# Moving the loads of a fused attention and MLP kernel to ScalarE's queue, the tail's exponentials to SBUF, and respacing the row-sum inverses

## The chip, the cores and the metric

The kernel runs on one NeuronCore of a Trainium2 chip. The core has five instruction streams that run side by side and meet at semaphores: TensorE (PE: matmuls, and PEld for its weight loads), VectorE (DVE), ScalarE (ACT), GpSimd (POOL) and SyncE (SP), which here only issues DMAs. Sixteen DMA engines move the data. The metric is the device time of one execution in microseconds (us); lower is better.

## The reference, cut to what matters

Attention over 4 batches, 8 heads, 576 positions and head size 64 with rotary positions, then a gated MLP with a mixing matrix over the positions, then a low-rank mixer and a wide MLP. The change lies in the attention.

```python
def _attn_ref(q, k, v):
    B, H, S, D = q.shape              # 4, 8, 576, 64
    ...
    q_rot, k_rot = (rotate(q), rotate(k))
    scores = (1.0 / np.sqrt(D)) * np.matmul(q_rot, k_rot.transpose(0, 1, 3, 2))
    scores = scores - np.max(scores, axis=-1, keepdims=True)
    attn = np.exp(scores)
    attn = attn / (np.sum(attn, axis=-1, keepdims=True) + 1e-09)
    return np.matmul(attn, v)

def _moe_ref(x, w_in, g_ln, w_sg, b_sg, w_out):
    h = gelu(x @ w_in); u, v = split(h)
    v_s = w_sg @ layernorm(v) * g_ln + b_sg
    return x + (u * v_s) @ w_out

def _moe2_ref(x, U, V, w_ch1, w_ch2):
    u = x + ((x.T @ U) @ V).T
    return u + np.maximum(u @ w_ch1, 0.0) @ w_ch2
```

The weights of the MLPs come as float64 and are turned to float32 on the chip.

## The kernel before

The attention runs head by head, 32 heads, in an order that is written by hand for all five engines. Time is counted in **ticks**: in each tick TensorE does one chunk `c` of 128 keys of one head `h` (five chunks a head, the fifth, the **tail**, has 64 keys), so head `h` has the ticks 5h to 5h + 4. In a tick `t` stand, in this order: the scores of chunk `t` (`scores`, four matmuls into a PSUM tile `st`), work left over for VectorE from the tick before (`lows`), one chunk of the row maxima of a head some ten ticks ahead (`row_max`, two matmuls into a PSUM tile `sm`, and VectorE's maximum over it into `MX`, L222), the product of the exponentials with the values of three ticks ago (`values`, L281), and then all that `later(t, ...)` has put down for this tick. Each engine works off its own list strictly in that order. `st` and `sm` share three PSUM buffers, so TensorE can write a new one only when ScalarE has taken the exponentials of an `st`, or VectorE the maximum of an `sm`, two or three tiles back.

What the change touches:

- **Loads.** `load(h)` (L138) brings the raw keys and queries of a head, 576 KB, at tick 5h - 30 into one of four buffers; `load_v(i)` (L143) brings the values of a pair of heads, in two transfers, at tick 10i - 16; `converted` (L348) brings a chunk of float64 weights (512 KB for most), one each 13 ticks, which ScalarE and VectorE convert from five ticks later on, one operation a tick (L71 to L75). All are issued by SP.
- **SP's other work** in the attention: copies that stack the rotated keys and queries on both halves of the partitions (`Q<-K`, `K<-K`, L164 to L170), a constant row (L174), the row of maxima that `scores` needs in its second two matmuls (`Q<-mt`, L226, issued when a head's maxima are all there, some four ticks ahead of its scores), and the inverses' four steps below. SP takes them in their order too: one that waits holds up all behind it.
- **Rotation.** GpSimd turns the raw keys and queries (`rope`, L149 to L151) from tick 5h - 23 on and makes the low part of the split keys (L168).
- **The tail's exponentials** (`scores`, L251 to L260). Four chunks of five go from PSUM through ScalarE's exponential to SBUF. The tail's are kept more precisely, as a rounded part and a rest: ScalarE takes the exponential in place in PSUM (L252), copies it rounded to SBUF (L254), and VectorE subtracts the two (L260) at the start of the next tick.
- **The inverses of the row sums** (`finish`). When the odd head of a pair is done, at tick t0 (10i + 12 for pair i), ScalarE has both heads' results in SBUF (`stage`, five buffers, L297). SP gathers their sums into a 128-partition tile (`collect`, rc, L312, at t0); `INVERSE = 4, 6, 9, 14` sets the ticks after t0 of the rest: GpSimd adds 1e-9 (L315), VectorE inverts (L318) and SP writes the result to DRAM (rr, L319), SP reads it back to 64 partitions (rb, L324), VectorE multiplies both heads by it (`apply`, L331, in two ticks).

After the attention come the MLP stages, in which Tile's scheduler orders all engines but TensorE.

Of the kernel before, what the change touches and what calls it, by code (L numbers as in the profile page):

```python
# [40 lines left out]

AHEAD, RAMP_FROM, RAMP, MAX_1, ROW, ROW_0, ROW_1 = 10, -1, 25, -1, 2, -8, -9

INVERSE = 4, 6, 9, 14

MATRIX, APART, CONVERT, ROWS = 12, 13, 5, (151, 159)

# [5 lines left out]
def tile_kernel(ctx: ExitStack, tc: tile.TileContext, qk, vv, tabs, w_in, g_ln, wsgT, b_sg, w_out, u_r, v_r, w1, w2, out):  # L53
# [32 lines left out]
    D = 64  # L86
# [48 lines left out]
    VSs = [p1.tile([P, 2, len(SPLITS), D + 1], F32R, name=f"VS_{i}") for i in range(4)]  # L135

    def load(h):
        nc.sync.dma_start(RAW[h % NR], qk[h // NHEAD, h % NHEAD].rearrange("c p s -> p c s"))  # L138

    def load_v(i):  # L140
        b, pr = divmod(i, NPAIR)
        for a in range(2):
            nc.sync.dma_start(VVs[i % 3][:, :, a, :D], vv[b, pr, :, :, a, :])  # L143

    def rope(e, h):

# [91 lines left out]
    def scores(h, c):  # L238
        kk = TS[c]
        K1, Q1, K2, Q2 = (t[h % NS] for t in (K1s, Q1s, K2s, Q2s))  # L240
        ps = psp.tile([P, 2, 512], F32, tag="ss", name=f"st{h}_{c}", bufs=3)
        for l, r, st in ((K1, Q1, True), (K2[0:D + 1], Q2, False)):
            for n in range(2):
                ns = slice(n * HALF, (n + 1) * HALF)
                nc.tensor.matmul(ps[:kk, n, :HALF], l[:, c * P:c * P + kk], r[:, ns], start=st, stop=not st)  # L245
        if c not in SPLITS:
            pc = p1.tile([P, S], F32, tag="pc", name=f"pc{h}_{c}", bufs=4)
            nc.scalar.activation(h2(pc[:kk]), ps[:kk, :, :HALF], AF.Exp, scale=0.125)  # L248
            PCS[h, c] = pc
            return  # L250
        pc = ps[:kk, :, :HALF]  # L251
        nc.scalar.activation(pc, pc, AF.Exp, scale=0.125)  # L252
        ph = p1.tile([P, S], F32R, tag="ph", name=f"ph{h}_{c}", bufs=3)
        nc.scalar.activation(h2(ph[:kk]), pc, AF.Copy)  # L254
        if kk == P:
            pl = p1.tile([P, S], F32R, tag="pl", name=f"pl{h}_{c}", bufs=2)
        else:
            pl = ph[D:P]
        PCS[h, c] = ph, pl
        lows.append(lambda: nc.vector.tensor_tensor(h2(pl), pc, h2(f(ph[:kk])), ALU.subtract))  # L260

    def values(h, c, t0):
        if c == 0:
# [3 lines left out]
        for n in range(2):  # L267
            ns = slice(n * HALF, (n + 1) * HALF)
            o = PVS[h][:D + 1, n, :HALF]
            if c in SPLITS:  # L270
                VS = VSs[h % 4]
                j = SPLITS.index(c)
                ph, pl = pc
                if kk == P:
                    pr = [(VS[:, 0, j], ph[:, ns]), (VS[:, 1, j], ph[:, ns]), (VS[:, 0, j], pl[:, ns])]
                else:
                    pr = [(VS[:, 0, j], ph[:, ns]), (VS[:, 1, j], ph[:, ns])]
            else:
                pr = [(VVs[(h // 2) % 3][:kk, c, h % 2], pc[:kk, ns])]
            for j, (l, r) in enumerate(pr):  # L280
                nc.tensor.matmul(o, l, r, start=(c == 0 and j == 0), stop=(c == NC - 1 and j == len(pr) - 1))  # L281
# [6 lines left out]
    def finish(h, t0):  # L288
# [27 lines left out]

        def invert():
            nc.vector.reciprocal(rc, rc)  # L318
            nc.sync.dma_start(rr, rc)  # L319

        def spread():
# [11 lines left out]
        def apply_last():  # L333
            nc.vector.tensor_tensor(X[b][:, pr], X[b][:, pr], RB[i], ALU.mult)
        later(t0, collect)
        for tick, fn in zip(INVERSE, (guard, invert, spread)):
            later(t0 + tick, fn)
        if i < NP - 1:
            for a in range(2):
                later(t0 + INVERSE[3] + a, lambda a=a: apply(a))  # L340
        else:
            later(t0 + INVERSE[3], apply_last)

    def converted(t0, src, n, use):

        raw = p1.tile([P, 512, 2], U32, tag="raw64", name="raw64", bufs=1)[:, :n]
        t = p1.tile([P, 512], F32, tag="t64", name="t64", bufs=1)[:, :n]
        later(t0, lambda: nc.sync.dma_start(raw.rearrange("p n w -> p (n w)"), src))  # L348
        for j, fn in enumerate(from_f64(t, raw) + use(t)):
            later(t0 + CONVERT + j, fn)  # L350

# [572 lines left out]
```

## Time and profile before

| | |
|---|---|
| median of 3 runs | 973.37 us (969.28 to 974.08) |
| the profiled execution | 976.05 us, span 974.0 us |
| busy share of the span | PE 96%, PEld 84%, DVE 53%, POOL 39%, ACT 35% |
| attention | some 12 to 325 us of the span |
| DMA engines, mean busy share | 0.54 to 0.75 in each 40 us up to 280 us |
| granted TensorE clock | 0.989 in the mean |

A row of the timeline is: start in us from the span's start, duration in us, engine, line, operation, out<-in, and in brackets the idle time before it with what ended it. SPq, ACTq and the like are an engine's sequencer: there the duration of a DMA row is the time that issuing took, not the transfer. The durations of single matmuls overlap, so that TensorE's pace is read from the distance between equal instructions of two heads and not from their sum.

### The profile page before, as it was taken

What the parts mean: (1) busy time and instruction counts of PE and PEld (TensorE: products, weight loads), DVE (VectorE), ACT (ScalarE), POOL (GpSimd) and SP (SyncE); (2) the same over time, 40 slices, a digit from 0 to 9 for tenths busy, and PEclk for the clock granted to TensorE, in tenths of its full rate; (3) what the DMA queues carried; (4) which work ended last, traced back from release to release, by engine and by line L of the source; (5) the groups of instructions that cost most, each with busy time, mean ns of one, the idle gap of its engine ahead of it and who ended that gap; (6) DMA issues with size and microseconds to landing.
All of it is one profiled execution on the core that took longest, in us unless ns stands there. A gap on an engine that the chain in (4) does not pass through costs nothing.

```text
span 974.0 us, 13234 instructions
## 1 busy us (share of the span) xinstructions
PE 938.5 (96%) x5211; PEld 817.4 (84%) x5212; DVE 515.3 (53%) x721; ACT 343.6 (35%) x549; POOL 377.1 (39%) x325
## 2 busy tenths in 40 slices
PE   6899988989999999999999899999999999999998
PEld 2687766767787898999999798899889988998897
DVE  7667776777775377344327946642552542212222
ACT  4466654655666463323215423221321221010010
POOL 7767866777761586231427533210210120000000
PEclk8999999999999999999999999999999999999999
DMA  5568676767751500000003001220220110000112
GB/s 177 143 181 199 174 178 160 206 158 172 190 128 49 159 28 1 1 1 1 23 22 109 23 23 60 91 66 1 87 87 1 65 44 1 1 1 21 60 40 75
DMA packets 58948, 78.00 MB, mean 80 GB/s; under 512 B 31403, under 2 KB 35270, under 8 KB 58886
## 3 DMA queue, kind: packets, MB, share of 16 engines
q1 hardware_dynamic: 58886, 77.16, 28.9%
q8 instruction: 41, 0.67, 0.3%
q14 instruction: 21, 0.17, 0.1%
HBM read 55.02 MB, written 4.79 MB: 61 GB/s over the span
## 4 chain that ended last, share of the span: by engine, by line
PE 76%; DVE 11%; DMA 5%; issue 3%; POOL 1%; SPq 1%; ACT 1%; DVEq 0%; ACTq 0%; POOLq 0%
PE a L551 21%; PE r L551 20%; PE pv L281 11%; PE st L245 6%; PE w L551 5%; PE sm L217 3%; PE m L551 3%; PE u L551 3%; PE v L551 3%; DVE MX L222 2%; DVE t L75 1%; DVE t L74 1%; DMA raw<-in_qk 1%; DMA g<-in_wsgT 1%; DVE t L72 1%
## 5 line engine op out<-in xcount | busy, mean ns | idle before, releaser
L222 DVE TENSOR_REDUCE MX<-sm 128x1 f32<-128x576 f32 (+1 forms) x160 | 119.3, 749 | 68.2 <-PE sm L217 42.1
L281 PE MATMUL pv<-pc,VV 128*65 128x288 f32 x512 | 146.7, 410 | 0.9 <-ACT stage L297 0.5
L245 PE MATMUL st<-Q,K 65*128 65x288 f32 (+3 forms) x640 | 126.7, 320 | 10.0 <-DVE MX L222 4.2
L245 PEld LDWEIGHTS st<-Q,K 65*128 65x128 f32 (+3 forms) x640 | 96.3, 180 | 24.4 <-DVE MX L222 7.3
L743 ACT ACTIVATE RH<-r 128x944 fp32r<-128x944 f32 (+1 forms) x38 | 35.7, 939 | 211.4 <-PE r L551 211.4
L744 DVE SCALAR_TENSOR_TENSOR RL<-r,RH 128x944 fp32r<-128x944 f32 (+1 forms) x38 | 42.4, 1117 | 126.3 <-ACT RH L743 126.2
L248 ACT ACTIVATE pc<-st 128x576 f32<-128x576 f32 x128 | 82.7, 647 | 66.8 <-PE st L245 63.6
L551 PE MATMUL a<-RH,setB 128*128 128x472 f32 (+1 forms) x320 | 95.6, 371 | 0.0
L281 PEld LDWEIGHTS pv<-pc,VV 128*65 128x65 f32 x512 | 69.1, 138 | 30.9 <-issue 1.0
L759 DVE TENSOR_TENSOR X<-a,X 128x416 f32<-128x416 f32 (+4 forms) x65 | 46.4, 745 | 91.0 <-PE a L551 91.0
L217 PE MATMUL sm<-K,Q 128*128 128x288 f32 (+1 forms) x320 | 78.3, 329 | 13.7 <-DVE MX L222 5.9
L551 PE MATMUL a<-RH,setA 128*128 128x472 f32 (+1 forms) x288 | 86.1, 370 | 0.0
L551 PE MATMUL r<-UH,setB 128*128 128x472 f32 (+1 forms) x256 | 76.4, 369 | 0.0
L551 PE MATMUL r<-UH,setA 128*128 128x472 f32 (+1 forms) x256 | 76.2, 370 | 0.0
L217 PEld LDWEIGHTS sm<-K,Q 128*128 128x128 f32 (+1 forms) x320 | 52.4, 184 | 22.9 <-DVE MX L222 8.1
L551 PEld LDWEIGHTS a<-RH,setB 128*128 128x128 f32 x320 | 60.2, 188 | 6.9
L515 POOL TENSOR_TENSOR setB<-t,setB 128x512 fp32r<-128x512 f32 x16 | 20.7, 1292 | 103.0 <-ACT setB L704 60.4
L551 PE MATMUL a<-RL,setB 128*128 128x472 f32 (+1 forms) x160 | 59.6, 372 | 0.0
L551 PEld LDWEIGHTS a<-RH,setA 128*128 128x128 f32 x288 | 54.1, 188 | 6.1
L551 PE MATMUL a<-RL,setA 128*128 128x472 f32 (+1 forms) x144 | 53.4, 371 | 0.0
L551 PEld LDWEIGHTS r<-UH,setA 128*128 128x128 f32 x256 | 48.1, 188 | 5.2
L551 PEld LDWEIGHTS r<-UH,setB 128*128 128x128 f32 x256 | 48.0, 188 | 5.2
(172 smaller groups left out, 1957.6 us busy)
## 6 DMA issues: line engine op xcount, KB each, us to landing
raw<-in_qk SPq DMA_DIRECT2D x31, 576.0 KB
Q<-K SPq DMA_DIRECT2D x87, 144.0 KB
raw<-in_w SPq DMA_DIRECT2D x24, 512.0 KB
VV<-in_vv SPq DMA_DIRECT2D x32, 160.0 KB
rb<-rr SPq DMA_DIRECT2D x15, 288.0 KB
K<-K SPq DMA_DIRECT2D x29, 144.0 KB
raw<-in_w_in SPq DMA_DIRECT2D x8, 512.0 KB
gt<-in_w SPq DMA_DIRECT2D x8, 512.0 KB
```

Of the source, the lines that this page charges most:

```text
L72: lambda: nc.vector.tensor_scalar(t, t, F64_LEAST, F64_MOST, ALU.max, ALU.min),
L74: lambda: nc.vector.scalar_tensor_tensor(tu, hi, 0xC0000000, tu, ALU.bitwise_and, ALU.bitwise_or),
L217: nc.tensor.matmul(ps[:TS[t], n, :HALF], Q1[:, t * P:t * P + TS[t]], K1[:, n * HALF:(n + 1) * HALF], start=True, stop=True)
L222: nc.vector.tensor_reduce(MXs[h % 2][:TS[t], t:t + 1], ps[:TS[t], :, :HALF], AX.XY, ALU.max)
L245: nc.tensor.matmul(ps[:kk, n, :HALF], l[:, c * P:c * P + kk], r[:, ns], start=st, stop=not st)
L248: nc.scalar.activation(h2(pc[:kk]), ps[:kk, :, :HALF], AF.Exp, scale=0.125)
L281: nc.tensor.matmul(o, l, r, start=(c == 0 and j == 0), stop=(c == NC - 1 and j == len(pr) - 1))
L515: return nc.gpsimd.tensor_tensor(out, a, b, ALU.subtract)
L551: nc.tensor.matmul(o, l, rr, start=(j == 0), stop=(j == n - 1))
L743: nc.scalar.activation(RH[:, s], ps[:, :, :WIDE[blk]], AF.Relu)
L744: nc.vector.scalar_tensor_tensor(RL[:, s], ps[:, :, :WIDE[blk]], 0.0, f(RH[:, s]), ALU.max, ALU.subtract)
L759: nc.vector.tensor_tensor(X[b][:, e2, xs], ps[:, :n, us], X[b][:, e2, xs], ALU.add)
```

## The change

Three things change. `load` from head 4 on, `load_v` from pair 2 on, and the loads of `converted` are issued by ScalarE in place of SP; they stand in ScalarE's list where they stood in SP's, at the end of their tick. The tail's exponential goes to a new SBUF tile `pt` (one buffer) instead of back to PSUM; the rounded copy and the subtraction then read `pt`, and `ph` has two buffers in place of three. The inverses' steps after `collect` come 6, 8, 9, 12 and 17 ticks after t0: the write to DRAM (`gather`) is a step of its own, one tick behind the inversion.

```diff
--- before.py
+++ after.py
@@ -41,7 +41,7 @@
 
 AHEAD, RAMP_FROM, RAMP, MAX_1, ROW, ROW_0, ROW_1 = 10, -1, 25, -1, 2, -8, -9
 
-INVERSE = 4, 6, 9, 14
+INVERSE = 6, 8, 9, 12, 17
 
 MATRIX, APART, CONVERT, ROWS = 12, 13, 5, (151, 159)
 
@@ -135,12 +135,12 @@
     VSs = [p1.tile([P, 2, len(SPLITS), D + 1], F32R, name=f"VS_{i}") for i in range(4)]
 
     def load(h):
-        nc.sync.dma_start(RAW[h % NR], qk[h // NHEAD, h % NHEAD].rearrange("c p s -> p c s"))
+        (nc.scalar if h >= NR else nc.sync).dma_start(RAW[h % NR], qk[h // NHEAD, h % NHEAD].rearrange("c p s -> p c s"))
 
     def load_v(i):
         b, pr = divmod(i, NPAIR)
         for a in range(2):
-            nc.sync.dma_start(VVs[i % 3][:, :, a, :D], vv[b, pr, :, :, a, :])
+            (nc.scalar if i > 1 else nc.sync).dma_start(VVs[i % 3][:, :, a, :D], vv[b, pr, :, :, a, :])
 
     def rope(e, h):
 
@@ -248,16 +248,12 @@
             nc.scalar.activation(h2(pc[:kk]), ps[:kk, :, :HALF], AF.Exp, scale=0.125)
             PCS[h, c] = pc
             return
-        pc = ps[:kk, :, :HALF]
-        nc.scalar.activation(pc, pc, AF.Exp, scale=0.125)
-        ph = p1.tile([P, S], F32R, tag="ph", name=f"ph{h}_{c}", bufs=3)
-        nc.scalar.activation(h2(ph[:kk]), pc, AF.Copy)
-        if kk == P:
-            pl = p1.tile([P, S], F32R, tag="pl", name=f"pl{h}_{c}", bufs=2)
-        else:
-            pl = ph[D:P]
-        PCS[h, c] = ph, pl
-        lows.append(lambda: nc.vector.tensor_tensor(h2(pl), pc, h2(f(ph[:kk])), ALU.subtract))
+        pt = p1.tile([D, S], F32, tag="pt", name=f"pt{h}", bufs=1)
+        nc.scalar.activation(h2(pt), ps[:kk, :, :HALF], AF.Exp, scale=0.125)
+        ph = p1.tile([P, S], F32R, tag="ph", name=f"ph{h}", bufs=2)
+        nc.scalar.activation(ph[:D], pt, AF.Copy)
+        PCS[h, c] = ph
+        lows.append(lambda: nc.vector.tensor_tensor(ph[D:], pt, f(ph[:D]), ALU.subtract))
 
     def values(h, c, t0):
         if c == 0:
@@ -270,11 +266,7 @@
             if c in SPLITS:
                 VS = VSs[h % 4]
                 j = SPLITS.index(c)
-                ph, pl = pc
-                if kk == P:
-                    pr = [(VS[:, 0, j], ph[:, ns]), (VS[:, 1, j], ph[:, ns]), (VS[:, 0, j], pl[:, ns])]
-                else:
-                    pr = [(VS[:, 0, j], ph[:, ns]), (VS[:, 1, j], ph[:, ns])]
+                pr = [(VS[:, 0, j], pc[:, ns]), (VS[:, 1, j], pc[:, ns])]
             else:
                 pr = [(VVs[(h // 2) % 3][:kk, c, h % 2], pc[:kk, ns])]
             for j, (l, r) in enumerate(pr):
@@ -316,6 +308,8 @@
 
         def invert():
             nc.vector.reciprocal(rc, rc)
+
+        def gather():
             nc.sync.dma_start(rr, rc)
 
         def spread():
@@ -333,19 +327,19 @@
         def apply_last():
             nc.vector.tensor_tensor(X[b][:, pr], X[b][:, pr], RB[i], ALU.mult)
         later(t0, collect)
-        for tick, fn in zip(INVERSE, (guard, invert, spread)):
+        for tick, fn in zip(INVERSE, (guard, invert, gather, spread)):
             later(t0 + tick, fn)
         if i < NP - 1:
             for a in range(2):
-                later(t0 + INVERSE[3] + a, lambda a=a: apply(a))
+                later(t0 + INVERSE[4] + a, lambda a=a: apply(a))
         else:
-            later(t0 + INVERSE[3], apply_last)
+            later(t0 + INVERSE[4], apply_last)
 
     def converted(t0, src, n, use):
 
         raw = p1.tile([P, 512, 2], U32, tag="raw64", name="raw64", bufs=1)[:, :n]
         t = p1.tile([P, 512], F32, tag="t64", name="t64", bufs=1)[:, :n]
-        later(t0, lambda: nc.sync.dma_start(raw.rearrange("p n w -> p (n w)"), src))
+        later(t0, lambda: nc.scalar.dma_start(raw.rearrange("p n w -> p (n w)"), src))
         for j, fn in enumerate(from_f64(t, raw) + use(t)):
             later(t0 + CONVERT + j, fn)
 
```

ScalarE's list around a tick that has a load, before (`raw` are the buffers of keys and queries and of float64 chunks, `VV` of values, `pc` and `ph` exponentials; the semaphores waited for stand in brackets):

```order
L252 ACTIVATE st_4_759<-st_4_759 64x2x288 [waits DVE_49,PE_49,Activation_49]
L254 ACTIVATE ph_4_765<-st_4_759 64x576 [waits Activation_49]
L182 ACTIVATE VS_123<-VV_118 128x64 [waits DMAHW0_49]
L248 ACTIVATE pc_0_782<-st_0_777 128x576 [waits PE_49]
L248 ACTIVATE pc_1_802<-st_1_797 128x576 [waits PE_49]
```

The same place now:

```order
L252 ACTIVATE pt_766<-st_4_761 64x576 [waits PE_49,Activation_49]
L254 ACTIVATE ph_768<-pt_766 64x576 [waits Activation_49]
L143 DMA VV_119<-in_vv 128x5x64 [waits DMAHW4_49]
L143 DMA VV_119<-in_vv 128x5x64 [waits DMAHW6_49]
L182 ACTIVATE VS_123<-VV_118 128x64 [waits DMAHW1_49]
L248 ACTIVATE pc_0_787<-st_0_782 128x576 [waits PE_49]
L138 DMA raw_93<-in_qk 128x2x576 [waits DMAHW0_49]
L342 DMA raw_162<-in_w_in 128x1024 [waits DMAHW2_49]
L248 ACTIVATE pc_1_807<-st_1_802 128x576 [waits PE_49]
```

Two loads of values stand between the tail's copy and the next exponential, and a load of keys and one of weights behind that; each load waits for a semaphore of the DMAs (DMAHW). In all, 28 loads of keys, 28 of values and 11 of weights have come into ScalarE's list.

SP's list at the end of a head, before:

```order
L174 DMA K_2_108<-less_one 1x16x36
L169 DMA K_3_99<-K_3_99 64x576
L170 DMA Q_3_104<-K_3_109 64x576
L138 DMA raw_93<-in_qk 128x2x576
L348 DMA raw_162<-in_w_in 128x1024
L226 DMA Q_1_112<-mt_809 1x5x128
L164 DMA Q_4_105<-K_4_100 64x576
L165 DMA Q_4_115<-K_4_100 64x576
L319 DMA rr_727<-rc_726 128x9
L174 DMA K_3_109<-less_one 1x16x36
```

The same heads now:

```order
L174 DMA K_2_108<-less_one 1x16x36
L169 DMA K_3_99<-K_3_99 64x576
L170 DMA Q_3_104<-K_3_109 64x576
L226 DMA Q_1_112<-mt_814 1x5x128
L164 DMA Q_4_105<-K_4_100 64x576
L165 DMA Q_4_115<-K_4_100 64x576
L174 DMA K_3_109<-less_one 1x16x36
```

The two loads ahead of the row of maxima (L226) are gone from SP's list, and the write of the inverses (L319, now L313) stands a head later, behind `L165` of the next head.

VectorE's list over the ticks in which a pair is multiplied by its inverses (X), before:

```order
L222 TENSOR_REDUCE MX_117<-sm_1_804 128x1
L225 CAST mt_809<-sm_1_804 5x128
L331 TENSOR_TENSOR X_66<-stage_440,rb_718 64x576
L222 TENSOR_REDUCE MX_117<-sm_2_833 128x1
L331 TENSOR_TENSOR X_66<-stage_529,rb_718 64x576
L222 TENSOR_REDUCE MX_117<-sm_3_849 128x1
L318 RECIPROCAL rc_726<-rc_726 128x9
L222 TENSOR_REDUCE MX_117<-sm_4_864 64x1
L260 TENSOR_TENSOR ph_4_862<-st_4_856,ph_4_862 64x576
L222 TENSOR_REDUCE MX_116<-sm_0_880 128x1
```

The same pair now:

```order
L222 TENSOR_REDUCE MX_117<-sm_4_866 64x1
L325 TENSOR_TENSOR X_66<-stage_441,rb_780 64x576
L256 TENSOR_TENSOR ph_864<-pt_862,ph_864 64x576
L222 TENSOR_REDUCE MX_116<-sm_0_883 128x1
L325 TENSOR_TENSOR X_66<-stage_531,rb_780 64x576
L310 RECIPROCAL rc_728<-rc_728 128x9
L222 TENSOR_REDUCE MX_116<-sm_1_904 128x1
L225 CAST mt_909<-sm_1_904 5x128
```

The two multiplications have come to stand on both sides of the tail's subtraction (L260, now L256), which reads `pt` in SBUF instead of `st` in PSUM, and the cast of the row of maxima follows them instead of preceding them. TensorE's list is the same but for names.

## Rows read from the trace of the kernel before

**Rows 1.** Windows: stretch, sum; busy us (count) of each engine; clock, DMA share, GB/s.

```profile
440.00:974.00 534.00, 526.01 (x2773) 479.28 (x2771) 223.03 (x306) 116.47 (x157) 95.73 (x66) 1.00 0.13 41
```

**Rows 2.** Timeline of PE: value products of the tails of nine heads.

```profile
42.29 0.90 PE L281 MATMUL pv<-ph,VS 128*65 128x288 f32 x4
...
130.59 0.90 PE L281 MATMUL pv<-ph,VS 128*65 128x288 f32 x4
143.18 0.90 PE L281 MATMUL pv<-ph,VS 128*65 128x288 f32 x4
152.32 0.90 PE L281 MATMUL pv<-ph,VS 128*65 128x288 f32 x4
166.33 0.90 PE L281 MATMUL pv<-ph,VS 128*65 128x288 f32 x4
...
201.50 0.91 PE L281 MATMUL pv<-ph,VS 128*65 128x288 f32 x4
209.99 0.90 PE L281 MATMUL pv<-ph,VS 128*65 128x288 f32 x4
223.99 0.90 PE L281 MATMUL pv<-ph,VS 128*65 128x288 f32 x4
...
301.02 0.90 PE L281 MATMUL pv<-ph,VS 128*65 128x288 f32 x4
```

**Rows 3.** The chain that ended last, in order of time: start, us, what.

```profile
125.95 7.39 DMA rb<-rr
...
153.65 7.71 DMA raw<-in_qk
```

**Rows 4.** Timeline of all engines in the stretches of three long gaps.

```profile
134.27 0.36 POOL L315 TENSOR_SCALAR rc<-rc 128x9 f32<-128x9 f32 x1 [6.98 <-DMA rc<-stage]
...
154.34 0.76 SPq L226 DMA_DIRECT2D Q<-mt  x1
161.47 0.51 PE L245 MATMUL st<-Q,K 65*128 65x288 f32 x2 [3.66 <-DMA raw<-in_qk]
...
209.43 0.76 DVE L222 TENSOR_REDUCE MX<-sm 128x1 f32<-128x576 f32 x1 [0.97 <-PE sm L220]
209.57 0.24 POOL L315 TENSOR_SCALAR rc<-rc 128x9 f32<-128x9 f32 x1 [3.95 <-DMA rc<-stage]
214.21 0.74 PE L245 MATMUL st<-Q,K 128*64 128x288 f32 x4 [0.76 <-DVE MX L222]
217.23 0.76 DVE L222 TENSOR_REDUCE MX<-sm 128x1 f32<-128x576 f32 x1
218.04 0.80 PE L245 MATMUL st<-Q,K 128*128 128x288 f32 x4 [1.86 <-DVE MX L222]
```

**Rows 5.** Waits: who waited for whom, us in all, times, longest.

```profile
POOL rc L315 <- DMA rc<-stage: 32.7, 11, 7.0
```

**Rows 6.** Waits of SP's queue, same columns.

```profile
SPq L319 <- DVE rc L318: 36.9, 15, 6.2
```

**Rows 7.** L260 and L331: duration ns min/median/max, first and last start, forms.

```profile
L260 DVE TENSOR_TENSOR ph<-st,ph x32: 750/752/752, 39.5 to 321.6; 64x576 fp32r<-64x576 f32 x32
L331 DVE TENSOR_TENSOR X<-stage,rb x30: 734/1053/1977, 77.4 to 325.8; 64x576 f32<-64x576 f32 x30
```

**Rows 8.** DVE's groups, 40 to 315 us: busy us, mean ns | idle.

```profile
L222 DVE TENSOR_REDUCE MX<-sm 128x1 f32<-128x576 f32 (+1 forms) x145 | 108.7, 749 | 64.6 <-PE sm L217 38.9 <-PE sm L220 23.9
L331 DVE TENSOR_TENSOR X<-stage,rb 64x576 f32<-64x576 f32 x27 | 32.7, 1211 | 2.8 <-DMA rb<-rr 2.4
```

**Rows 9.** Timeline of SP, 177 to 189 us: issue of a pair's values.

```profile
187.78 1.28 SPq L143 DMA_DIRECT2D VV<-in_vv  x2
```

**Rows 10.** Timeline of ACT, 179 to 183 us: a tail, the next exponential.

```profile
179.66 0.64 ACT L254 ACTIVATE ph<-st 64x576 fp32r<-64x576 f32 x1
...
180.72 0.65 ACT L248 ACTIVATE pc<-st 128x576 f32<-128x576 f32 x1 [0.28 <-PE st L245]
```

**Rows 11.** Timeline of PE, 179 to 183 us: the maxima two chunks on.

```profile
182.28 0.42 PE L217 MATMUL sm<-K,Q 128*128 128x288 f32 x2
```

## The prediction

> **What bounds the kernel now.** I read the windows first. From 440 us on TensorE is busy 526 of 534 us at a granted clock of 1.00, which is its upper level of 2.4 GHz [rows 1]; the change touches nothing there, so all of it is decided in the attention. Next the timeline of TensorE: the product of a tail's exponentials with its values comes once a head. Where nothing disturbs it the distance is 8.49 us (201.50 to 209.99), 1.70 us a tick. From 42.29 to 301.02 lie 28 heads in 258.73 us; 28 x 8.49 would be 237.7. So 21.0 us are lost there, and three heads hold most of it [rows 2]: gap A (130.59 to 143.18) 12.59 us, 4.10 too long; gap B (152.32 to 166.33) 14.01, 5.52 too long; gap C (209.99 to 223.99) 14.00, 5.51 too long. Together 15.1; the other 25 heads lose 5.9.
>
> What ended last there is told by the chain and the timeline. In A a return of the inverses (rb) issued at 125.95 took 7.39 us to land [rows 3], and VectorE stood in front of its multiplication; GpSimd then waited 6.98 us for the next pair's sums [rows 4]. In B a row of maxima, issued at 154.34, stood behind a load of keys issued at 153.65 that took 7.71 us [rows 3, 4]; SP's list has a float64 chunk between the two. TensorE's scores waited 3.66 us. In C GpSimd waited 3.95 us for the sums, its rotation came later and denser beside VectorE, and a conversion fell into the same ticks. VectorE's multiplications (L331) were among its longest: from the maximum at 209.43 to that at 217.23, two ticks on, it took 7.80 us against 3.40; TensorE waited 0.76 and 1.86 us for maxima [rows 4].
>
> So what is late is small transfers behind large ones in SP's list, and engines that wait in order on one step of the inverses. Over the run GpSimd waited 32.7 us at L315 for sums [rows 5] and SP 36.9 us at L319, in 15 waits, for VectorE's inversion, with loads and rows of maxima queued behind it [rows 6].
>
> **The loads on ScalarE's queue.** The gain: a row of maxima or a return no longer stands behind a head's keys and a chunk in the same list, and 67 issues leave SP (28 of keys, 28 of values, 11 chunks). In B this takes away the wait, 5.52 us. In A the same holds for the return, 4.10 us. The bound is from nothing (the 16 DMA engines are shared anyway) to both gaps whole; I take both, since the short transfers there were late only with a long one just ahead in their own list.
>
> The cost: two loads of values are 1.28 us of a sequencer on SP [rows 9]; I take ScalarE's price to be the same. They stand behind the tail's copy (179.66, 0.64 us) and ahead of the next exponential (180.72, idle 0.28 before) [rows 10]. That exponential could start at 180.44; behind the issues it starts at 181.72 and ends, with its 0.65, at 182.37. The tile of maxima that needs its PSUM buffer was written at 182.28 [rows 11], so TensorE is 0.09 us late at most on this reckoning: 14 pairs x 0.07 = 1.0 us. Lower bound 0, if the sequencer issues while the engine still works; upper bound the whole 1.28 - 0.28 = 1.0 x 14 = 14 us. Single loads of keys and chunks lie in ticks in which ScalarE has only a 0.65 us exponential in 1.70 us, and cost nothing so; without that cover each is 0.64. Each load also waits for the semaphore of an earlier DMA, often one of SP's; queued behind it are the exponentials, and TensorE waits for these. I put that at nothing, since the lists of loads run ahead of their use, and price it in the third rival.
>
> **The inverses' steps.** Adding 1e-9 comes two ticks later, 3.4 us, against a mean wait of 32.7 / 11 = 3.0 us [rows 5]; the write to DRAM comes a tick behind the inversion instead of directly after it, so SP meets it done. GpSimd's bunching that led to C goes. C's other half, a float64 conversion in the ticks of the multiplications, stays possible, now with other pairs, because chunks come each 13 ticks and pairs each 10. I take half of C, 2.75 us, and a quarter of the scattered 5.9, 1.5 us; the bounds are 0 and 11.4.
>
> **The tail in SBUF, and where the multiplications now stand.** The old subtraction reads one operand from PSUM and takes 0.750 to 0.752 us in all 32 cases; the multiplication, of the same size with two SBUF operands, takes 0.734 to 1.977 [rows 7], 1.21 in the mean [rows 8], and its long ones in C fell where GpSimd's delayed work ran beside it. The new subtraction is of the second kind: 0.46 us more in the mean, 32 x 0.46 = 14.7 us more for VectorE. The Trainium skill says the same in "SBUF — State Buffer", section "Who interferes with whom": a VectorE instruction with at most one SBUF input does not contend with GpSimd, one with two does when GpSimd reads SBUF. By that rule, the trace agrees, this edit speaks against itself, and it gives the first rival.
>
> VectorE is not the bound in the mean: it idles 64.6 us ahead of 145 maxima [rows 8], 0.45 us a tick. But the new steps 17 and 18 put the two multiplications on both sides of the subtraction, with the next pair's inversion behind them. Two ticks, 3.40 us, then hold two maxima (1.50), two multiplications (2.42), the subtraction (1.21) and the inversion (an estimate of 0.2, from L315's 0.24 on the same tile [rows 4]): 5.3 us, 1.9 over. What TensorE tolerates is read from C: 7.80 - 3.40 = 4.40 us over, of which it waited 0.76 + 1.86 = 2.62, so about 1.8 us are covered. In the mean that just holds; as each of the three takes 0.73 to 1.98, the pairs scatter by some 0.7 us to either side and about half of them are late. I take 0.35 us a pair, 14 x 0.35 = 5 us. Lower bound 0 (all three at 0.734: 3.9 us, 0.5 over, covered); upper bound all three at 1.98: 7.6 us, 4.2 over, 2.4 late, 34 us, which needs GpSimd beside each one. In return the PSUM buffer of the tail is released by ScalarE rather than VectorE; I count nothing for it, since no long gap above hung on that subtraction.
>
> **The sum.** Against the profiled execution: 976.05 - 4.10 - 5.52 - 2.75 - 1.5 + 1.0 + 5 = 968.2 us. That execution lies 2.7 above the median of 973.37, so the forecast for the median is 965.5 us. With all 21.0 us gone and nothing added it is 976.05 - 21.0 - 2.7 = 952.4. A measurement of this kernel can tell about 0.5% from no change: faster is below 968.5, slower above 978.2.
>
> **Rivals.** First, VectorE becomes late in the crowded ticks. For it: two more all-SBUF operands in a place that has a 1.9 us excess already. Against it: most heads before keep 8.49 us with multiplications of 1.21 in the mean. If each pair is late by a further 0.65 us (operands at 1.43 instead of 1.21), that is 9.1 us: 974.6, no change.
>
> Second, the loads change their queue but not the lateness of the small transfers, because all share 16 engines. Then A's and B's 9.6 us come back: 965.5 + 9.6 = 975.1, no change. For it: the load in B is itself slow, 7.71 us. Against it: the small transfers are late only behind such a load in their own list. The Trainium skill speaks for this rival ("DMA: Bandwidth & Descriptors", section "Issuing engines are not separate DMA queues"): DMAs started by different engines run on the same 16 engines, and starting them from several saves only sequencer time. No run here yet has large loads on a second queue.
>
> Third, the slower side: ScalarE is held by its own loads. A load waits for an earlier DMA of SP's list, which may wait for VectorE's inversion; SP's 15 waits there are 36.9 / 15 = 2.5 us each [rows 6]. If half of that, 1.2 us, reaches an exponential in each of 14 pairs, that is 17 us, since ScalarE's idle there is but 0.28 us: 965.5 + 17 = 982.5, slower. It decides from 0.9 us a pair on (12.7 us to 978.2). Against it: the write now stands a tick behind the inversion in SP's list, so that list should run with less lag.
>
> **How the numbers follow.** The forecast with its own range of 955 to 972 has 0.57; the first rival 0.17, the second 0.11, the third 0.15. Faster is the forecast's part below 968.5 (0.47) and a share of the first two where their price is half (0.06): 0.53. Slower is the third (0.13) and a strong form of the first (0.03): 0.16. No change is the rest, 0.31. The range for 8 in 10 is 955 to 979: it takes in the two rivals that end at no change, and leaves most of the third out.
>
> **What would show it.** Right: head distances at 8.50 us with no gap of 12 to 14; the waits of L315 and of the write of inverses nearly gone; returns and rows of maxima landing in under 4 us; TensorE's waits for maxima in the ticks of the multiplications below 0.4 us a pair. The tail's subtraction should move from 0.75 towards 1.2 us. Wrong: TensorE's waits for maxima in each pair, with subtractions and multiplications near 2 us (first rival); rows of maxima that still take 7 us (second); ScalarE's waits on a DMA with exponentials that start late behind a load (third).

## The result and the profile after

The changed kernel takes 989.10 us in the median (987.81 to 989.90) against 973.48 in the same session: a ratio of 1.0147, 95% interval 1.0116 to 1.0178 (the ratio is estimated from all runs and is not the quotient of the two medians, which is 1.0160). It is slower by some 15 us, where the forecast had 965.5 and a range up to 979. Two single executions far above the rest, one of before (1550.85 us) and one of the run guard_late below (5276.57 us), count in the medians of their sessions but not in the ratios.

TensorE's timeline, the same product of a tail once a head as in [rows 2]:

```profile
45.03 0.90 PE L273 MATMUL pv<-ph,VS 128*65 128x288 f32 x4
...
156.37 0.91 PE L273 MATMUL pv<-ph,VS 128*65 128x288 f32 x4
168.93 0.90 PE L273 MATMUL pv<-ph,VS 128*65 128x288 f32 x4
...
311.38 0.90 PE L273 MATMUL pv<-ph,VS 128*65 128x288 f32 x4
```

Twenty-eight heads, from 45.03 to 311.38, take 266.35 us against 258.73: in these two executions 7.6 us of the loss lie here, 2.7 before the first of these products (45.03 against 42.29). The granted clock is not what sets the two apart there: from 40 to 320 us it is 1.00, the upper level of 2.4 GHz, in both, but for 0.91 in 160 to 180 and in 220 to 240 us, also in both. Ahead of 40 us it is lower in the changed kernel (0.76 and 0.81 in the first two stretches of 20 us, against 0.83 and 0.91); whether that makes the 2.7 us was not tried. The gaps of 12 to 14 us have not gone (156.37 to 168.93 is 12.56), and more heads are a little late: 12 of the 28 are over 9.50 us, against 4.

What TensorE waited for in the attention (who waited for whom, us in all, times, longest):

```profile
PE st L245 <- DMA Q<-mt: 8.6, 6, 2.3
PE sm L217 <- DVE MX L222: 4.4, 6, 1.7
PE st L245 <- DVE mt L225: 3.6, 4, 1.2
```

A row of maxima that has not landed (`Q<-mt`) leads the list. Two more waits of the same scores, 2.1 us (`Q<-K`) and 1.3 us (a chunk), are put down to other transfers but end where the row lands, which makes 12.0 us in 8 places. Before, two such waits, also put down to loads, made 4.8 us: the 3.66 us of gap B [rows 4] and this one:

```profile
83.66 0.50 PE L245 MATMUL st<-Q,K 65*128 65x288 f32 x2 [1.14 <-DMA raw<-in_w_in]
```

When a DMA lands can be read, roughly, from the semaphore events, matched to the issues in order. Seven of the eight rows waited for landed 5.6 to 6.9 us after their issue, and five of these had been issued as soon as their cast was done. The mean of all rows is 3.44 us, against 3.16 before. So these rows are late mostly on their way and not in SP's list. Behind the rows come VectorE's maxima and the cast of the row (L225). What GpSimd and SP waited for, and the two lines that change their place or operands:

```profile
POOL rc L307 <- DMA rc<-stage: 12.3, 5, 6.3
```

```profile
SPq L313 <- DVE rc L310: 10.0, 1, 10.0
```

```profile
L256 DVE TENSOR_TENSOR ph<-pt,ph x32: 751/884/1947, 41.1 to 332.0; 64x576 fp32r<-64x576 f32 x32
```

```profile
L325 DVE TENSOR_TENSOR X<-stage,rb x30: 734/752/1948, 84.3 to 341.0; 64x576 f32<-64x576 f32 x30
```

GpSimd's wait for the sums has fallen from 32.7 to 12.3 us [rows 5], SP's 15 waits at the write of the inverses, 36.9 us, to a single one of 10.0 [rows 6]. The tail's subtraction (L256) now takes 0.751 to 1.947 us in place of 0.752 [rows 7]; over 40 to 325 us its mean is 1.22. So these steps moved as foreseen, and the time went elsewhere. Two places show where. First the DMA issues around 152 us, SP's and ScalarE's (of the rows "VV" two loads of values, "ph" the tail's copy, on ScalarE itself, "raw" a chunk and keys, "rb" the return):

```profile
153.78 0.46 SPq L318 DMA_DIRECT2D rb<-rr  x1
...
156.29 0.50 SPq L169 DMA_DIRECT2D K<-K  x1
156.84 0.59 SPq L170 DMA_DIRECT2D Q<-K  x1
157.52 0.77 SPq L226 DMA_DIRECT2D Q<-mt  x1
```

```profile
151.87 0.69 ACT L254 ACTIVATE ph<-pt 64x576 fp32r<-64x576 f32 x1
151.87 1.25 ACTq L143 DMA_DIRECT2D VV<-in_vv  x2
...
153.20 0.60 ACTq L342 DMA_DIRECT2D raw<-in_w_in  x1
...
153.88 0.43 ACTq L138 DMA_DIRECT2D raw<-in_qk  x1
```

The chain of waits (start, us, what), and the scores that waited in TensorE's timeline:

```profile
157.52 6.50 DMA Q<-mt
```

```profile
164.15 0.82 PE L245 MATMUL st<-Q,K 65*128 65x288 f32 x2 [2.29 <-DMA Q<-mt]
```

Within 2.5 us the values, a chunk, the keys and the return are started on two queues, all of it ahead of the low copies and of the row of maxima (157.52), 2.5 KB that land 6.50 us later; the scores that need it stand idle for 2.29 us. In SP's list of before the return stood behind that row; its new tick, 12 instead of 9, puts it in front. Second, VectorE at 203 us, and TensorE:

```profile
202.93 1.75 DVE L325 TENSOR_TENSOR X<-stage,rb 64x576 f32<-64x576 f32 x1
204.70 1.87 DVE L256 TENSOR_TENSOR ph<-pt,ph 64x576 fp32r<-64x576 f32 x1
206.60 0.76 DVE L222 TENSOR_REDUCE MX<-sm 128x1 f32<-128x576 f32 x1
207.39 1.07 DVE L325 TENSOR_TENSOR X<-stage,rb 64x576 f32<-64x576 f32 x1
...
209.24 0.27 DVE L225 CAST mt<-sm 5x128 fp32r<-5x128 f32 x1
```

```profile
209.65 0.77 PE L245 MATMUL st<-Q,K 128*128 128x288 f32 x4 [1.16 <-DVE mt L225]
```

Multiplication, subtraction, maximum and multiplication take most of the 6.3 us from 202.93 to the cast at 209.24, which before preceded them; the inversion and one more maximum (0.21 and 0.69 us) lie between. GpSimd worked beside them without a pause from 202.04 to 210 us. TensorE waits 1.16 us for the PSUM buffer that the cast reads.

### The profile page after: what moved, and what is told of

Same layout as the page of the kernel before. It is cut to its first block, busy times and chain, and to the rows that moved or that the text cites. A ratio compares the mean times of both kernels' runs of the same rounds, so it can differ in the third digit from the quotient of the medians.

```text
span 986.6 us, 13250 instructions
## 1 busy us (share of the span) xinstructions
PE 941.5 (95%) x5212; PEld 818.8 (83%) x5212; DVE 521.7 (53%) x721; ACT 345.9 (35%) x549; POOL 381.1 (39%) x325
## 3 DMA queue, kind: packets, MB, share of 16 engines
q10 hardware_dynamic: 27568, 26.05, 10.5%
## 4 chain that ended last, share of the span: by engine, by line
PE 71%; DVE 11%; DMA 8%; issue 4%; POOL 3%; ACT 1%; SPq 1%; ACTq 0%; DVEq 0%; POOLq 0%
PE a L545 20%; PE r L545 20%; PE pv L273 8%; PE st L245 5%; PE w L545 4%; DMA Q<-mt 3%; PE m L545 3%; PE sm L217 3%; PE u L545 3%; PE v L545 2%; DVE MX L222 2%; DMA raw<-in_qk 1%; DVE t L75 1%; DVE ph L256 1%; DVE t L74 1%
## 5 line engine op out<-in xcount | busy, mean ns | idle before, releaser
L245 PE MATMUL st<-Q,K 65*128 65x288 f32 (+3 forms) x640 | 128.7, 322 | 15.7 <-DMA Q<-mt 8.6
L217 PE MATMUL sm<-K,Q 128*128 128x288 f32 (+1 forms) x320 | 78.4, 330 | 15.9 <-DVE MX L222 9.1
L150 POOL TENSOR_TENSOR raw<-raw,tab 128x576 f32<-128x576 f32 x31 | 50.6, 1632 | 5.2 <-DMA raw<-in_qk 5.2
```

The source lines that it names most:

```text
L150: lambda: e.tensor_tensor(raw[:, 1], raw[:, 1], tab[:, 1], ALU.mult),
L217: nc.tensor.matmul(ps[:TS[t], n, :HALF], Q1[:, t * P:t * P + TS[t]], K1[:, n * HALF:(n + 1) * HALF], start=True, stop=True)
```

## The experiments

Each run has a name, in brackets. Each ratio is that of its executions to those of the kernel before in the same session, with a 95% interval; medians of before lay between 972.73 and 974.96 us. The intervals are 0.2 to 0.5% to either side, so a difference of less than some 3 us between two kernels of this list tells nothing.

**Undoing each part.** In the expectations Q, S and I stand for the second queue, ScalarE held by its issues, and the inverses' ticks.

Loads back on SP (no_loads):

```
-        (nc.scalar if h >= NR else nc.sync).dma_start(RAW[h % NR], ...
+        nc.sync.dma_start(RAW[h % NR], ...
-            (nc.scalar if i > 1 else nc.sync).dma_start(VVs[i % 3]...
+            nc.sync.dma_start(VVs[i % 3]...
-        later(t0, lambda: nc.scalar.dma_start(raw...
+        later(t0, lambda: nc.sync.dma_start(raw...
```

> The changed kernel with keys, values and float64 chunks issued by SyncE again (tail in SBUF and the spread inverses stay). Three theories. Q: the loads in a second queue fall into the same few us as SyncE's copies and rows, share the DMA engines with them, and the rows of maxima land late (in the changed kernel the copies K<-K take 5.5 us in the median against 2.5). S: ScalarE's own issues hold up its exponentials. I: the return of the inverses, now 12 ticks behind the collection, falls into the same tick as the values and one ahead of the keys, whichever queue these are in. Q and S expect 962 to 972 us here; I expects 982 to 990.

Measured: 983.96 us, 1.0109 (1.0067 to 1.0150). Most of the loss stays; Q and S are not the main cause. With the new ticks the loads on ScalarE seem to cost 5.1 us (989.10 to 983.96; the intervals of the two kernels overlap), which without them they do not, as the loads alone show below. Why is not shown: the waits on rows, 14.2 us in 9 places in this profile, are not fewer.

The inverses' old ticks (no_inverse):

```
-INVERSE = 6, 8, 9, 12, 17
+INVERSE = 4, 6, 6, 9, 14
```

> The changed kernel with the inverses' steps at their old ticks (guard 4, inversion and write 6, return 9, multiplications 14 and 15 after the collection); loads on ScalarE and the tail in SBUF stay. Q and S expect no more than a few us of gain, 983 to 990 us. I expects the loss gone: 970 to 977.

Measured: 975.14 us, 1.0014 (0.9990 to 1.0038). The loss is gone: it is the ticks, as I has it. This run moves all of them back, so it does not tell the return from the multiplications.

The tail in PSUM again (no_tail):

```
-        pt = p1.tile([D, S], F32, tag="pt", name=f"pt{h}", bufs=1)
-        nc.scalar.activation(h2(pt), ps[:kk, :, :HALF], AF.Exp, scale=0.125)
+        pc = ps[:kk, :, :HALF]
+        nc.scalar.activation(pc, pc, AF.Exp, scale=0.125)
...
-        lows.append(lambda: nc.vector.tensor_tensor(ph[D:], pt, f(ph[:D]), ALU.subtract))
+        lows.append(lambda: nc.vector.tensor_tensor(h2(pl), pc, h2(f(ph[:kk])), ALU.subtract))
```

> The changed kernel with the tail's exponential in PSUM again and the subtraction reading PSUM. Q, S and I expect the time of the changed kernel within 3 us, 986 to 990 (the subtraction costs VectorE 0.3 us a head in the mean and is hidden). A theory that VectorE became late in the crowded ticks (the prediction's first rival) expects 973 to 980.

Measured: 980.85 us, 1.0089 (1.0060 to 1.0117). Q, S and I all missed here; the theory of VectorE's lateness came nearest, 0.85 us off its range. With the new ticks the tail's place costs 8.2 us (989.1 to 980.85). The subtraction is 0.47 us shorter in PSUM in the mean (0.75 against 1.22), not 0.3. The edit also gives `ph` its third buffer back, but the buffers held nobody up: in the changed kernel ScalarE waited at `pt` for TensorE's scores alone.

**One part alone, on the kernel before.** The loads (only_loads; the first diff, reversed):

> The kernel before with nothing but the loads of keys (from head 4), values (from pair 2) and float64 chunks moved to ScalarE. Q and S expect the whole loss or more from this part alone: 984 to 992 us. I expects 965 to 975, as the return then stands three ticks ahead of the values.

Measured: 973.75 us, 1.0004 (0.9982 to 1.0025). The loads neither gain nor cost anything that can be told, so Q and S fall as causes by themselves. With no_inverse (these loads and the tail) that leaves the tail in SBUF 1.4 us where the inverses keep their ticks, which is within the noise. A long gap as C stays in its profile, with the same signs (GpSimd's wait for sums, a long multiplication):

```profile
206.11 0.24 POOL L315 TENSOR_SCALAR rc<-rc 128x9 f32<-128x9 f32 x1 [5.40 <-DMA rc<-stage]
...
208.08 1.95 DVE L331 TENSOR_TENSOR X<-stage,rb 64x576 f32<-64x576 f32 x1
...
214.58 0.79 PE L245 MATMUL st<-Q,K 128*128 128x288 f32 x4 [1.54 <-DVE MX L222]
```

The new ticks alone (only_inverse). In this expectation R is the theory that the return's place costs the time, V that the multiplications' place does, by making VectorE late:

```
-INVERSE = 4, 6, 9, 14
+INVERSE = 6, 8, 9, 12, 17
...
+        def gather():
             nc.sync.dma_start(rr, rc)
```

> The kernel before with nothing but the new ticks of the inverses (6, 8, 9, 12, 17); loads on SyncE, tail in PSUM. R: 978 to 985 us, the larger part of the loss. V: 974 to 979, as the subtraction that reads PSUM is not drawn out beside GpSimd.

Measured: 981.30 us, 1.0083 (1.0053 to 1.0114). The ticks cost some 7.5 us without the two other parts. R fits, and TensorE's waits agree: the row of maxima is waited for, and the cast (`mt`), behind the multiplications in this kernel too, is not:

```profile
PE st L245 <- DMA Q<-mt: 10.7, 6, 4.2
...
PE st L245 <- DVE mt L225: 0.2, 1, 0.2
```

**Which of the inverses' steps?** In the next three, on the changed kernel, only the numbers of INVERSE differ: 6, 8, 9, 14, 17 (return_14), then 4, 6, 6, 9, 17 (return_9), then 4, 6, 6, 12, 17 (return_12).

> The changed kernel with one number changed: the return of the inverses 14 ticks after the collection instead of 12, so that in SyncE's list it follows the row of maxima instead of preceding the low copies and that row; the multiplications stay at 17 and 18. Theory R: what costs is the place of the return (288 KB) ahead of the copies and the row: 972 to 979 us. Theory V: what costs is the place of the multiplications, around the tail's subtraction and ahead of the cast of the row of maxima, where VectorE is late: 985 to 991 us, as the changed kernel.

Measured: 1010.26 us, 1.0363 (1.0314 to 1.0411). A miss for both theories, through my own edit: the three ticks from 14 to 17 are too few for the return, and VectorE, with all else queued behind, waited for it:

```profile
DVE X L325 <- DMA rb<-rr: 31.2, 10, 6.1
```

> The changed kernel with the inverses' first steps at their old ticks (guard 4, inversion and write 6, return 9) and only the multiplications late, at 17 and 18. R: 973 to 978 us, as the kernel with all the old ticks (975.1). V: 983 to 990 us.

Measured: 981.96 us, 1.0077 (1.0049 to 1.0105), 6.8 us over no_inverse, from which only the multiplications differ. V holds, just under its range. TensorE's waits of this kernel, and then of no_inverse:

```profile
PE st L245 <- DVE mt L225: 10.0, 11, 1.4
PE sm L217 <- DVE MX L222: 5.9, 4, 4.0
...
PE st L245 <- DMA Q<-mt: 0.9, 2, 0.8
```

```profile
PE sm L217 <- DVE MX L222: 3.5, 5, 1.3
PE st L245 <- DMA Q<-mt: 3.5, 4, 1.5
...
PE st L245 <- DVE mt L225: 1.0, 2, 0.6
```

The wait on the cast rises from 1.0 us in 2 places to 10.0 us in 11, not quite one a pair. (Of the 5.9 us on maxima one wait of 4.0 lies at 29.4 us, ahead of the first scores; every kernel has it, and it is in the list of cheap_mult below too.)

> The same with the return at 12: guard 4, inversion and write 6, return 12, multiplications 17 and 18. R: 984 to 990 us, as the changed kernel, since the return stands where that has it. V: the same as with the return at 9, 983 to 990; the two kernels together tell R from V. If 973 to 978, it is the late adding of 1e-9 and inversion that cost.

Measured: 981.90 us, 1.0077 (1.0048 to 1.0106). The median shows no cost of moving the return on top, but the waits of its profile changed places: on rows of maxima 8.9 us in 7 places against 2.9 in 3 (`Q<-K` counted in), on the cast less:

```profile
PE st L245 <- DMA Q<-mt: 7.0, 6, 3.5
PE st L245 <- DVE mt L225: 6.6, 7, 1.4
```

The kernel is 7.2 us below the changed kernel, whose adding, inversion and write stand later.

**Taking each cost away in the changed kernel.** Multiplications that read one tile (cheap_mult), and then the place of the multiplications (mult_19). D is the theory that the return itself delays the row in the DMA queues:

```
-            nc.vector.tensor_tensor(X[b][rows, pr], STAGE.pop(h - 1 + a)[:D], RB[i][:, a], ALU.mult)
+            nc.vector.tensor_scalar(X[b][rows, pr], STAGE.pop(h - 1 + a)[:D], RB[i][:, a, 0:1], None, ALU.mult)
```

> The changed kernel in which the two multiplications per pair read one SBUF operand and one number per partition (the first column of the returned inverses) instead of two tiles; ticks, waits and the transfer of the return stay. It leaves out the division by each column's own sum. Theory V (the multiplications around the tail's subtraction make VectorE late with the cast of the row of maxima, which holds a PSUM buffer and the row): 975 to 983 us, and TensorE's waits on the cast (3.6 us in the changed kernel) and on the row Q<-mt (8.6 us) shrink. Theory D (the late return itself delays the row in the DMA queues): 986 to 990.

Measured: 983.54 us, 1.0091 (1.0060 to 1.0121): 5.6 us less. The waits on the cast fall to 0.9 us, as V has it, but those on the row of maxima grow from 8.6 to 11.4; V's limit of 983 was just missed, and there is a second cost:

```profile
PE st L245 <- DMA Q<-mt: 11.4, 9, 2.3
PE sm L217 <- DVE MX L222: 8.3, 7, 4.0
PE st L245 <- DVE mt L225: 0.9, 1, 0.9
```

```
-INVERSE = 6, 8, 9, 12, 17
+INVERSE = 6, 8, 9, 12, 19
```

> The changed kernel with the multiplications at 19 and 20 ticks instead of 17 and 18: they then stand behind the cast of the row of maxima again, as in the kernel before, which had them at 14 and 15 (the same place within a head). V: 976 to 983 us. D: 986 to 990. A loss beyond that would come from the five buffers of results, the oldest of which is then free only one tick before it is written again.

Measured: 981.88 us, 1.0072 (1.0047 to 1.0098): 7.2 us less, V again, and no wait on the cast is left; the row of maxima still costs:

```profile
PE st L245 <- DMA Q<-mt: 9.1, 6, 3.3
PE sm L217 <- DVE MX L222: 5.6, 7, 1.7
PE pv L273 <- ACT stage L289: 3.3, 6, 1.4
```

Then the second cost, on cheap_mult (small_return). G is the theory that the later adding of 1e-9 (`guard`) and inversion cost the time:

```
-nc.sync.dma_start(RB[i].rearrange("p a s -> p (a s)"), rr.to_broadcast([D, 2 * S]))
+nc.sync.dma_start(RB[i][:, :, :1], rr.rearrange("p (a s) -> p a s", a=2)[:, :, :1].to_broadcast([D, 2, 1]))
```

> The changed kernel with cheap multiplications (983.5 us), and the return brings only the first column of each head to 64 partitions, some 0.5 KB instead of 288; its place in SyncE's list, its wait and the other ticks stay. It leaves out the division by each column's own sum. D: 973 to 978 us, and TensorE's waits on the row Q<-mt (11.4 us with the whole return) fall under 4 us. G: 982 to 985.

Measured: 977.01 us, 1.0024 (1.0006 to 1.0042): 6.5 us less than with the whole return at the same place in the same list. D holds in time, and the difference is not VectorE's wait for the return, since cheap_mult had none up to 330 us. The waits on the row fall to 6.0 us only, not under 4:

```profile
PE st L245 <- DMA Q<-mt: 6.0, 5, 3.7
```

INVERSE = 6, 8, 9, 14, 19 (both_late), the whole transfer, but behind the row of maxima:

> The changed kernel with the return at 14 and the multiplications at 19 and 20: both then stand within a head where the kernel before has them, the return behind the row of maxima, the multiplications behind the cast; adding, inversion and write stay at 6, 8 and 9. D: 973 to 978 us. G: 981 to 984, as with the multiplications alone moved (981.9).

Measured: 978.15 us, 1.0025 (1.0008 to 1.0042): 3.7 us below mult_19, just over D's range. The wait on the row is down to 3.1 us, but another has come, on ScalarE's copy into a buffer of results that the late multiplications free too late (ScalarE waits 14.1 us for them):

```profile
PE pv L273 <- ACT stage L289: 6.1, 7, 2.5
PE st L245 <- DMA Q<-mt: 3.1, 2, 2.4
```

INVERSE = 6, 7, 7, 9, 14 (guard_late):

> The changed kernel with loads on ScalarE and the tail in SBUF, the return at 9 and the multiplications at 14 and 15 as before, but the adding at 6 and inversion and write at 7. D: 973 to 977 us, as with all old ticks (975.1). G: 979 to 984.

Measured: 973.31 us, 0.9979 (0.9957 to 1.0001). Adding two ticks and inverting and writing one tick later, alone, cost nothing: G falls, as far as this goes (the changed kernel inverts at 8 and writes at 9).

**What is left.** On the kernel before, with the tail in PSUM: the steps 4, 6, 7, 9, 14 (loads_gather7) and 5, 7, 8, 10, 15 (loads_later1) with all loads on ScalarE; only keys and chunks there (keys_chunks); and 6, 7, 7, 9, 14 with all loads (loads_guard) or with keys and chunks (keys_guard).

> The kernel before with the loads on ScalarE and the write of the inverses one tick behind the inversion (4, 6, 7, 9, 14), so that SyncE is not held at it (it waits 46.9 us there with the loads alone moved); multiplications at their old place, tail in PSUM. If the waits of SyncE's queue are what is left: 966 to 972 us. If they are covered: 973 to 975.

Measured: 975.05 us, 0.9989 (0.9965 to 1.0012), no difference. The edit did not take SP's waits away (44.7 us in its profile at the write), so it does not tell whether they are covered.

> The same with every step one tick later: guard 5, inversion 7, write 8, return 10, multiplications 15 and 16. V: the multiplications come one tick nearer to the tail's subtraction but both still stand ahead of it: 968 to 976 us. If the return, now 10 ticks behind the collection, matters: 976 to 982.

Measured: 979.81 us, 1.0053 (1.0031 to 1.0074). One tick later for all of it costs half a per cent. The time lies in the range for the return, but the profile, of its fastest execution (972.99 us), shows 0.4 us of waits on rows; which of the steps does it was not tried further.

> The kernel before with only the loads of keys and of float64 chunks on ScalarE; values stay on SyncE, the inverses and the tail as before. If the values' two issues between a tail and the next exponential take back what the other loads give: 968 to 972 us. If loads on a second queue give nothing here: 972 to 975.

Measured: 972.89 us, 0.9986 (0.9965 to 1.0007): no difference that can be told.

> The kernel before with all three kinds of loads on ScalarE and the steps 6, 7, 7, 9, 14 (adding two ticks later, inversion and write one); return, multiplications and tail as before. If the tail in SBUF still costs its 1.4 us without the late multiplications: 970 to 973 us. If it makes no difference: 972 to 975.

Measured: 972.37 us, 0.9990 (0.9971 to 1.0009). Both ranges hold it, so it decides nothing; guard_late, the same with the tail in SBUF, has 0.9979, so that no cost of the tail shows at these ticks.

> The same with the values' loads on SyncE. If the gains of both add up (0.9979 and 0.9986 of the kernel before): 969 to 972 us. If not: 972 to 975.

Measured: 969.40 us, 0.9973 (0.9950 to 0.9997). This one, keys and chunks on ScalarE with adding and inverting later, is ahead of both kernels, by 0.3%, with an interval that just leaves out no change; as one of 18 variants it can be chance.

## Why the prediction was wrong

The terms of the forecast, as the runs have them:

| term | forecast | measured |
|---|---|---|
| loads on ScalarE's queue | -9.6 + 1.0 | 0 (only_loads: 1.0004); with the new ticks perhaps +5.1 (no_loads) |
| tail in SBUF, multiplications around it | +5 | +1.4, within noise (no_inverse), and +6.8 (return_9) |
| waits taken away by the new ticks | -4.25 | no gain told: guard_late 1.8 below no_inverse, intervals overlap |
| return ahead of the row of maxima | not counted | none told with the early write (return_12), +6.5 with the late one (small_return) |

Built up part by part, the runs go from 973.75 us (loads) to 975.14 (tail in SBUF), 981.96 (multiplications at 17), 981.90 (return at 12) and 989.10 (adding, inversion and write late as well). Two steps, 6.8 and 7.2 us, make nearly all of the loss.

**The loads: the step that failed first.** "In B this takes away the wait, 5.52 us. In A the same holds for the return, 4.10 us" took the long transfers in the same list for the cause and gave both gaps whole. The rows of before allowed less: in the whole attention VectorE waited 2.4 us for returns [rows 8], TensorE 3.66 for B's row, and a conversion stood in A's ticks as in C's, one of its steps drawn out to 1.89 us:

```profile
133.37 0.75 DVE L331 TENSOR_TENSOR X<-stage,rb 64x576 f32<-64x576 f32 x1 [2.39 <-DMA rb<-rr]
...
139.22 1.89 DVE L74 SCALAR_TENSOR_TENSOR t<-raw,t 128x512 uint32<-128x512 uint32 x1
```

Loads alone moved nothing, and the interval allows at most 0.18%, 1.8 us, of gain. In the profile of only_loads 28 heads take 255.8 us against 258.7, with gaps A and B gone, but the medians agree: a long gap in one execution is not a loss that every execution has at that place. Executions of before ranged from 968 to 981 us (all but that one), and I summed the three gaps of one of them as if they were fixed. The second rival named a mechanism that fits, that transfers share the DMA engines whichever queue they stand in. What speaks for it beside the time: by the semaphore events (matched to issues in order, so roughly) the copies `K<-K` land 4.6 us after their issue in the mean in only_loads, against 3.0 before, and the keys 5.7 against 4.7. The Trainium skill has this in "DMA: Bandwidth & Descriptors", section "Issuing engines are not separate DMA queues", and the measured 1.0004 agrees with it; the forecast should have gone by it. The rival's sign, rows of maxima that still take 7 us, came too: seven that TensorE waited for took 5.6 to 6.9. The third rival, ScalarE held by its own issues, falls with the same run: 67 loads stood in its list, and that cost nothing that can be told (+1.0 was forecast, from 14 x 0.07 where the reckoning had 0.09). In the changed kernel TensorE waited 0.2 us for ScalarE in the whole attention: the loads of values start while the tail's copy still runs (both at 151.87 above), and what sticks out was covered.

**The return: the step left out.** Under the inverses' steps the prediction priced only the adding and the write, and elsewhere the place of the multiplications. The fourth number, 12 for 9, moves a transfer of 288 KB in SP's list from behind the row of maxima and the next high copies to ahead of the low copies and the row. It was in the diff, and it had no term. Making that transfer small at its place gives back 6.5 us (measured with cheap multiplications). The traces agree over all runs: in the eight kernels with the return at 12 TensorE waited 6.0 to 15.2 us for rows of maxima, the 6.0 with the small return, and in the twelve others 0.4 to 4.8.

**The multiplications: right in kind, a little small.** Two multiplications around an all-SBUF subtraction, 5.3 us of work in the 3.4 us of two ticks, were to cost 5 us, with up to 34, and in the first rival 9.1 more; they cost 5.6 (made cheap), 6.8 (moved alone) and 7.2 (moved away). That the first rival is at work shows in the cure by any of its ingredients: the subtraction in PSUM gave 8.2 us back, and with it the wait on the cast is 0.2 us (3.6 in the changed kernel). What was wrong is who waits: not the maxima, as forecast, but the cast of the row, which had stood ahead of the multiplications and now stands behind them, and which holds a PSUM buffer. The price of the subtraction was right: 1.22 us in the mean against 1.21. The Trainium skill's rule on two SBUF inputs beside GpSimd ("SBUF — State Buffer", "Who interferes with whom") is borne out by 0.751 to 1.947 us in place of 0.752, and by the place above, where 1.75 and 1.87 us fell beside a busy GpSimd.

**The waits that went: no gain seen.** GpSimd's 32.7 us and SP's 36.9 us fell as foreseen, and no run shows a gain from it that can be told. In guard_late GpSimd's waits on those sums are 15.9 us in the attention and the longest of the 28 heads takes 10.5 us, so that gap C is gone too; its time is that of before within its interval. SP still waits 51.7 us at the write there; no run takes SP's waits away with the return and the multiplications at their old ticks, so what they are worth alone stays open.

**Open.** The costs are not additive. With the early write (return_12) the median shows no cost of the return at 12 ticks over the return at 9; with the late write its size cost 6.5 us. In return_12 SP waited 29.0 us in 13 waits at the write, nearly as in the kernel before, and so issued the return and the copies behind it at other times. That this lag keeps the transfers apart was not tried, and the 8.9 us of waits on rows there rather speak against it; its waits on the cast were fewer, 6.6 us against 10.0 in return_9. Nor was it settled why the loads on ScalarE seem to cost 5.1 us with the new ticks, nor why loads_later1 is slower.

## What to carry to other kernels

When a step is moved, write down for each of its instructions what now stands behind it in its queue: a multiplication that passes a small cast, or a large transfer that passes a small one, cost more here than the removed waits gave back. Long waits on engines that are not the bound, and long gaps of a single profiled execution, are no measure of what removing them gives; move one part alone and time it. Before counting on a second queue, ask whether the late transfer waits for its issue or for the DMA engines.

## What the runs showed of the hardware

I had not expected a multiplication with one tile and one number per partition to be that much shorter: 0.514 us in the median against 0.752 with two tiles of the same size, though it too reached 1.652 at times (the line's duration ns min, median, max, first and last start, in cheap_mult):

```profile
L325 DVE TENSOR_SCALAR X<-stage,rb x30: 499/514/1652, 84.4 to 335.5; 64x576 f32<-64x576 f32 x30
```

The other surprise was that a row of 2.5 KB took 6.50 us with 1984 KB started on both queues in the 5.7 us ahead of it (320 of values, 512, 576, 288 and two copies of 144), and that 67 loads in ScalarE's list, at 0.43 to 0.63 us each in the rows above, changed the time by less than 0.3% where the inverses kept their ticks.
